# Attention and a gelu layer in one kernel: batch 1's first chunk asked for ahead, W_in in quarters, and another order of the first batch's steps

## The chip, the cores and the metric

The kernel runs on one core of one Trainium2 chip. Its time is the device time of one launch in microseconds. Before the change three runs took 426.42, 427.21 and 431.62 us; the median is 427.21. The core has a tensor engine (PE), a vector engine (DVE), a scalar engine (ACT), GpSimd (POOL) and a sync engine (SP). Each works through its own queue of instructions in order, and semaphores tie the queues together. Sixteen DMA engines carry the data.

## The reference

```python
q_n, k_n = (rmsnorm(q, g_q), rmsnorm(k, g_k))        # q, k, v: 8 batches x 12 heads x 448 tokens x 64
scores = scale * np.matmul(q_n, k_n.transpose(0, 1, 3, 2))
attn = np.exp(scores - np.max(scores, axis=-1, keepdims=True))
attn = attn / (np.sum(attn, axis=-1, keepdims=True) + 1e-09)
x = np.matmul(attn, v).transpose(0, 2, 1, 3).reshape(3584, 768)
h = x @ w_in                                          # 768 x 2048
g = 0.5 * h * (1.0 + np.tanh(c * (h + 0.044715 * h * h * h)))
out = g @ w_out                                       # 2048 x 768
```

All inputs and the output are float32. The kernel casts v and the weights to bfloat16 while they are loaded.

## The kernel before

Each batch goes through the same stages: q and k are squared, summed and normed (`square`, `total`, `rsqrt`, `normed`), transposed, multiplied to scores, and passed through an exponential; the exponentials are multiplied with v; the result x goes through the first matrix product and gelu; and the second matrix product of batch b runs inside the attention of batch b + 1, in whose queue its matmuls fill the gaps. A batch's twelve heads are cut into three chunks (`NCH`) of four heads, and a chunk into two pairs j = 0 and 1.

From batch 2 on these stages follow a regular plan. Batch 0 has nothing before it that could hide its loads and its norms, so its steps, and those that prepare batch 1, stand in a list written out by hand, `FRONT`. The function `front` carries out one step after the other, and each engine gets its instructions in the order of that list. A step is named by what it does and by a number; a letter behind a colon names the engine (A for ACT, D for DVE, P for POOL):

- `sq`, `sk` square a pair of q or of k of batch 0 (i = 2 x chunk + pair); `tq`, `tk` sum the squares on DVE; `rs` makes the reciprocal roots of both on ACT (a logarithm and an exponential); `nq`, `nk` multiply by them; `tpq`, `tpk` transpose on PE; `cq`, `ck` copy the transposed pair from PSUM to SBUF.
- `s0` to `s20` are the scores of batch 0, seven tiles for each chunk; `e0` to `e20` are their exponentials on ACT.
- For each of the six pairs of heads, `su` sums the exponentials on PE (by a product with ones), `st`, `rc`, `rb` transpose the sum, take its reciprocal and transpose it back on DVE, `xp` multiplies with v on PE, and `xt` scales the result on DVE. `su` writes the one bank of PSUM called o, which `st` frees.
- `z` puts idle products with zeros into PE's queue (z403: three of them, in the bank of pair 4).
- `ma`, `mc`, `md` are parts of the first matrix product, which reads `win` (W_in) two blocks of 128 columns at a time; `g0` to `g8` are the gelus.
- `v0`, `v1`, `v2` load batch 0's v: v0 its main part, v1 and v2 the last 64 tokens; `V0` to `V2` the same for batch 1. `w` loads a part of W_in's columns, `o0` to `o3` quarters of W_out. POOL issues all of these, among its own arithmetic.
- `L10`, `L11`, `L12` load chunks 0, 1, 2 of q and k of batch 1; SP issues them, six DMAs for a chunk.
- `Sq`, `Sk`, `Tq`, `Tk`, `Rs`, `Nq`, `Nk`, `Tp`/`TP`, `Cq`, `Ck` prepare batch 1 as the small letters do batch 0. `GELU` and `EXP` load ACT's tables, and `U` adds a third place in PSUM for scores.

The scores and the first product take turns in two, after `U` three, places in PSUM. Raw q and k have four buffers each (`rawqk`); before the list starts, batch 0's three chunks are loaded, and two pairs of tiles are allocated that nothing uses. The parts of W_in are loaded by `w_in_part(i, n)`, the i-th of n equal ranges of columns.

Of the kernel before, what the change touches and what calls it, by code (L numbers as in the profile page):

```python
# [8 lines left out]
F32 = mybir.dt.float32  # L9
# [7 lines left out]
def kernel(  # L17
# [12 lines left out]
    B, H, S, D = q.shape  # L30
# [21 lines left out]
    rawqk = ctx.enter_context(tc.tile_pool(name="rawqk", bufs=4))  # L52
# [29 lines left out]
    gcol = consts.tile([128, 1], F32)  # L82
# [3 lines left out]
    shift = consts.tile([128, 1], F32)  # L86
# [22 lines left out]
    def load_q(b, c):  # L109
        t = rawqk.tile([P, CH, NQ, D], F32, tag="rawq", name="rawq")  # L110
        raws["q", b, c] = t
        return [
            lambda j=j: nc.sync.dma_start(
                t[:, 2 * j:2 * j + 2],
                q[b, head(c, j):head(c, j) + 2].rearrange("h (p t) d -> p h t d", t=NQ),
            )
            for j in range(2)
        ]
# [6 lines left out]
    def load_k(b, c):  # L125
        t = rawqk.tile([128, 2, NS, D], F32, tag="rawk", name="rawk")
        raws["k", b, c] = t

        def main(j):
            h = head(c, j)  # L130
            nc.sync.dma_start(
                t[:, :, 4 * j:4 * j + NK],
                k[b, h:h + 2, :SM].rearrange("a (p t) d -> p a t d", t=NK),
            )

        def last(j):
            h = head(c, j)
            nc.sync.dma_start(t[own(j), :, NK], k[b, h:h + 2, SM:].rearrange("a p d -> p a d"))
# [25 lines left out]
    def sq_tile(n, flat):  # L164
        if n == "q":
            return flat[:P].rearrange("p (h t d) -> p h t d", h=CH, t=NQ)
        return flat[:, :2 * NS * D].rearrange("p (a s d) -> p a s d", a=2, s=NS)
# [29 lines left out]
    def total(b, c, n, j=None):  # L197
        nc.vector.reduce_sum(stat(ssq[b % 3], b, c, n, j), view(n, sqs[n, b, c], j), axis=AX.X)  # L198

    def rsqrt(b, c=slice(0, NCH), at=slice(0, NU)):  # L200
        if b not in rinvs:
            rinvs[b] = smp.tile([128, NCH, NU], F32, tag="rinv", name="rinv")
        lg = smp.tile([128, NCH, NU], F32, tag="lg", name="lg")
        nc.scalar.activation(
            lg[:, c, at], ssq[b % 3][:, c, at], AF.Ln, scale=1.0 / D, bias=eps
        )
        nc.scalar.activation(rinvs[b][:, c, at], lg[:, c, at], AF.Exp, scale=-0.5)  # L207
# [124 lines left out]
    def bank():  # L332
        return ps_o.tile([128, 512], F32, tag="o", name="o")
# [223 lines left out]
    nc.scalar.preload_act_table_set(EXP_SET)  # L557
    loads(0, 1)
    loads(0, 2)

    for _ in range(2):
        rawqk.tile([P, CH, NQ, D], F32, tag="rawq", name="rawq")
        rawqk.tile([128, 2, NS, D], F32, tag="rawk", name="rawk")
    nc.vector.memset(eps, 1e-6)
    nc.vector.memset(ones, 1.0)
    nc.vector.memset(rows, 1.0)
# [10 lines left out]
    free = g.rearrange("p f s -> p (f s)")  # L577
    for i, (n, c) in enumerate((n, c) for c in range(NCH) for n in "qk"):
        sqs[n, 0, c] = sq_tile(n, free[:, i * 2048:(i + 1) * 2048].bitcast(F32))

    def w_in_part(i, n):
        m = d_ff // n
        nc.gpsimd.dma_start(
            win[:, :, i * m:(i + 1) * m],
            moe_w_in[:, i * m:(i + 1) * m].rearrange("(c p) f -> p c f", p=128),
        )
# [34 lines left out]
    def front(step):  # L621
        what, _, eng = step.partition(":")
        name, i = what.rstrip("0123456789"), what[len(what.rstrip("0123456789")):]
        i, eng = int(i or 0), ENG.get(eng)
        c, j = i // 2, i % 2
        n = name[-1]
        if name in ("sq", "sk"):
            square(0, c, n, eng, ("pair", j))
        elif name in ("tq", "tk"):
            total(0, c, n, j)  # L630
        elif name == "rs":
            rsqrt(0, c, slice(14 * j, 14 + 16 * j))
        elif name in ("nq", "nk"):
            normed(0, c, n, j, eng)
        elif name in ("tpq", "tpk"):
            tps[n, i] = trans(0, i, n, turn[0], name)
        elif name == "cq":
            place_q(0, i, tps["q", i], eng)
        elif name == "ck":
            place_k(0, i, tps["k", i], eng)  # L640
        elif name == "U":
            third()
        elif name == "gcol":
            gains()
        elif name == "shift":
            shifts()
        elif name == "s":
            exps[i] = scores(0, *TILES[i])
        elif name == "e":
            exps[i]()  # L650
        elif name == "z":
            hp, m = divmod(i, 100)
            if hp not in sums_at:
                sums_at[hp] = bank()
            idle(m, sums_at[hp][:, :S])
        elif name == "su":
            pair_products(0, i, 0, sums_at.get(i))
        elif name == "st":
            recip_in()
        elif name == "rc":  # L660
            recip()
        elif name == "rb":
            recip_out(i)
        elif name == "xp":
            pair_products(0, i, 1, ps_m.tile([128, 512], F32, tag="mm", name="ox"))
        elif name == "xt":
            pair_x(0, i)
        elif name == "v":
            load_v(0, i)
        elif name == "w":  # L670
            w_in_part(i, 2)
        elif name == "V":
            load_v(1, i)
        elif name == "o":
            w_out_part(i // 2, slice(i % 2 * nf // 2, (i % 2 + 1) * nf // 2))
        elif name == "L":
            loads(*divmod(i, 10))
        elif name in ("Sq", "Sk"):
            square(1, i, n, eng)
        elif name in ("Tq", "Tk"):  # L680
            total(1, i, n)
        elif name == "Rs":
            rsqrt(1, slice(0, 2))
        elif name in ("Nq", "Nk"):
            normed(1, i // 10, n, i % 10, eng)
        elif name == "Tp":
            tps["Q", i] = trans(1, i, "q", ps_o, "o")
            tps["K", i] = trans(1, i, "k", ps_m, "mm")
        elif name == "TP":
            tp = place("tp").rearrange("p a s -> p (a s)").bitcast(BF16)  # L690
            tps["Q", i], tps["K", i] = (
                trans(1, i, n, tp[:, 1024 * a:1024 * (a + 1)]) for a, n in enumerate("qk"))
        elif name == "Cq":
            place_q(1, i, tps["Q", i], eng)
        elif name == "Ck":
            place_k(1, i, tps["K", i], eng)
        elif name in ("GELU", "EXP"):
            nc.scalar.preload_act_table_set(EXP_SET if name == "EXP" else GELU_SET)
        elif name in ("ma", "mc", "md"):
            fs = [2 * i, 2 * i + 1] if i < 7 else [i + 7]  # L700
            cs = {"ma": range(4), "mc": [4], "md": [5] if i < 3 else range(HP)}[name]
            mm1(0, fs, cs, act=False)
        elif name == "g":
            gelu(0, [2 * i, 2 * i + 1] if i < 7 else [i + 7])
        else:
            raise ValueError(step)

    FRONT = """
        sq0:A tq0 sk0:A tk0 sq1:P gcol rs0 shift nq0:P tq1 sk1:A tk1 tpq0 sq2:A v0 nk0:D rs1 cq0:D
        tpk0 tq2 sk2:A z3 v1 ck0:A tk2 v2 s0 nk1:D rs2 s1 w0 nq1:D e0 tpk1 sk3:D w1 tpq1 e1 s2 tk3  # L710
        z5 sq3:P ck1:D e2 cq1:D nk2:P tq3 s3 sq4:A s4 nq2:D rs3 tpk2 e3 tq4 nq3:P tpq2 z1 ck2:D e4
        cq2:D s5 nk3:D su0 e5 sk4:D L10 s6 tk4 sq5:P tpq3 e6 st0 tpk3 s7 sk5:P tq5 rs4 su1 rc0 e7
        rb0 nk4:P s8 ck3:D nq4:P s9 e8 st1 tpk4 cq3:D xp0 e9 ck4:D tk5 tpq4 xt0 s10 rs5 s11 cq4:D
        e10 xp1 nq5:P rc1 rb1 e11 s12 nk5:P xt1 su2 e12 L11 L12 s13 st2 tpq5 e13 tpk5 s14 rc2
        Sk0:P xp2 ck5:D e14 rb2 s15 xt2 su3 cq5:A Sq0:P e15 U Tk0 s16 xp3 e16 st3 s17 rc3 Tq0 s18
        e17 z403 rb3 e18 s19 su4 xt3 e19 s20 st4 xp4 e20 o0 rc4 rb4 ma0 GELU o1 xt4 Sq1:P su5 xp5
        V0 V1 st5 V2 Sk1:P rc5 mc0 rb5 ma1 xt5 Tq1 o2 o3 md0 mc1 Tk1 g0 md1 ma2 g1 EXP mc2 md2 md3
        Rs0 GELU Nq00:D Nk00:D Sk2:D g2 Tp0 md4 g3 Nk01:D Sq2:D Ck0:A Cq0:A Nk11:D md5 g4 Nq01:D
        Tq2 Nk10:P Nq10:P Tk2 Tp1 g5 Nq11:P md6 Ck1:D Cq1:A md7 g6 TP2 Ck2:D Cq2:D md8 TP3 Ck3:D
        Cq3:D g7 g8  # L720
"""
    for step in FRONT.split():
        front(step)
# [146 lines left out]
```

## Time and profile before

| | |
|---|---|
| median of three runs | 427.21 us (426.42 to 431.62) |
| the profiled execution | 429.53 us |
| its span, first to last instruction | 427.8 us |
| mean granted clock of PE | 0.992 |
| PE busy | 410.6 us, 96% of the span |
| ACT, DVE, POOL busy | 296.8, 279.0, 133.7 us |
| read from HBM, written to it | 45.61 MB, 11.01 MB |

The span and what lies around it (1.7 us) make the profiled execution's time. A busy share is an average over the whole span. The list `FRONT` covers the first 64 us of it, so the first 64 us are to be read on their own: which engine waits there, for whom, and what the DMA engines carry meanwhile.

### The profile page before, as it was taken

What the parts mean: (1) busy time and instruction counts of PE and PEld (TensorE: products, weight loads), DVE (VectorE), ACT (ScalarE), POOL (GpSimd) and SP (SyncE); (2) the same over time, 40 slices, a digit from 0 to 9 for tenths busy, and PEclk for the clock granted to TensorE, in tenths of its full rate; (3) what the DMA queues carried; (4) which work ended last, traced back from release to release, by engine and by line L of the source; (5) the groups of instructions that cost most, each with busy time, mean ns of one, the idle gap of its engine ahead of it and who ended that gap; (6) DMA issues with size and microseconds to landing.
All of it is one profiled execution on the core that took longest, in us unless ns stands there. A gap on an engine that the chain in (4) does not pass through costs nothing.

```text
span 427.8 us, 9133 instructions
## 1 busy us (share of the span) xinstructions
PE 410.6 (96%) x3733; PEld 232.7 (54%) x3733; DVE 279.0 (65%) x452; ACT 296.8 (69%) x400; POOL 133.7 (31%) x139
## 2 busy tenths in 40 slices
PE   7697999999999999999999999999999999999996
PEld 2232555565555655556555655556555655556563
DVE  5985676798769856787468836787387742683010
ACT  5786659678898678776877668776777558774300
POOL 6737660016000375009520375008430370000000
PEclk9988999999999999999999999999999999999999
DMA  8999998954991098915992097925972061120022
GB/s 194 222 225 231 203 199 158 220 152 100 174 251 41 2 181 202 167 53 116 196 181 73 14 201 142 188 61 104 199 103 71 10 124 38 43 72 2 0 76 74
DMA packets 96298, 54.15 MB, mean 127 GB/s; under 512 B 63744, under 2 KB 91264, under 8 KB 96256
## 3 DMA queue, kind: packets, MB, share of 16 engines
q1 hardware_dynamic: 71392, 41.67, 42.9%
q0 software_dynamic: 24544, 11.80, 21.1%
q8 instruction: 29, 0.48, 0.5%
q10 hardware_dynamic: 320, 0.10, 0.1%
q14 instruction: 13, 0.11, 0.1%
HBM read 45.61 MB, written 11.01 MB: 132 GB/s over the span
## 4 chain that ended last, share of the span: by engine, by line
PE 81%; DMA 7%; ACT 5%; DVE 5%; issue 1%; SPq 1%; POOL 0%; DVEq 0%; ACTq 0%; POOLq 0%
PE o L418 33%; PE hh L391 25%; PE o L349 10%; DMA rawk<-in_k_dram 7%; PE sc L312 6%; PE h L391 4%; PE sc L302 1%; ACT g L400 1%; ACT ex L316 1%; DVE ss L198 1%; DVE sq L183 1%; ACT exr L316 1%; DVE es L328 1%; ACT sq L181 1%; DVE st L356 1%
## 5 line engine op out<-in xcount | busy, mean ns | idle before, releaser
L418 PE MATMUL o<-wout,g 128*64 128x384 bf16 (+1 forms) x1664 | 157.8, 326 | 0.0
L316 ACT ACTIVATE ex<-sc,shift 128x896 bf16<-128x896 f32 x144 | 136.2, 1013 | 6.4 <-PE sc L312 6.4
L391 PE MATMUL hh<-xT,win 128*64 128x448 bf16 (+1 forms) x924 | 133.2, 353 | 0.1
L418 PEld LDWEIGHTS <-g 128*64 128x64 bf16 (+1 forms) x1664 | 98.7, 109 | 49.1 <-issue 3.8
L391 PEld LDWEIGHTS <-win 128*64 128x64 bf16 (+1 forms) x1062 | 86.2, 105 | 59.1 <-issue 3.6
L400 ACT ACTIVATE g<-hh 128x896 bf16<-128x896 f32 x56 | 49.4, 916 | 48.7 <-PE hh L391 48.7
L198 DVE TENSOR_REDUCE ss<-sq 128x14 f32<-128x896 f32 (+2 forms) x43 | 47.4, 1124 | 30.4 <-ACT sq L181 18.5
L440 ACT COPY osb<-o 128x384 f32<-128x384 f32 x51 | 24.7, 484 | 49.2 <-PE o L418 49.1
L727 POOL COPY mark<-es 1x1 bf16<-1x1 bf16 x6 | 1.1, 178 | 170.2 <-DVE es L330 170.2
L356 DVE STREAM_TRANSPOSE st<-o 128x448 f32<-128x448 f32 x48 | 31.1, 648 | 28.2 <-PE o L349 28.1
L221 POOL TENSOR_TENSOR nrmq<-rawq,rinv 112x512 bf16<-112x512 f32 x36 | 38.8, 1093 | 6.0 <-ACT rinv L207 6.0
L312 PE MATMUL sc<-qT,kT 64*128 64x448 bf16 x288 | 39.4, 358 | 1.3 <-ACT exr L316 0.8
L330 DVE TENSOR_TENSOR es<-ex 128x896 bf16<-128x896 bf16 x42 | 26.3, 627 | 17.6 <-ACT ex L316 17.6
L221 POOL TENSOR_TENSOR nrmk<-rawk,rinv 128x384 bf16<-128x384 f32 (+1 forms) x34 | 35.4, 1055 | 5.0 <-issue 3.4
L349 PE MATMUL o<-ex,vb 128*64 128x448 bf16 x252 | 31.2, 353 | 1.2 <-DVE st L356 1.2
L364 DVE STREAM_TRANSPOSE rb<-rc 128x448 f32<-128x448 f32 x48 | 30.9, 645 | 1.6
L274 DVE TENSOR_SCALAR kT<-kT,gcol 128x896 bf16<-128x896 bf16 x19 | 21.8, 1146 | 13.4 <-DMA kT<-nrmk 13.4
L328 DVE TENSOR_TENSOR es<-es,exr 64x896 bf16<-64x896 bf16 x42 | 26.0, 618 | 3.0 <-ACT exr L316 1.6
L330 DVE TENSOR_TENSOR es<-es,ex 128x896 bf16<-128x896 bf16 x42 | 25.6, 609 | 2.6 <-ACT ex L316 0.7
L374 DVE TENSOR_TENSOR xT<-o,rb 128x448 bf16<-128x448 f32 x42 | 25.9, 616 | 0.7
L316 ACT ACTIVATE exr<-sc,shift 128x896 bf16<-128x896 f32 x24 | 24.5, 1019 | 0.6 <-PE sc L302 0.5
L312 PEld LDWEIGHTS <-kT 64*128 64x128 bf16 x288 | 10.1, 94 | 25.1 <-issue 19.3
(79 smaller groups left out, 333.3 us busy)
## 6 DMA issues: line engine op xcount, KB each, us to landing
rawq<-in_q_dram SPq DMA_DIRECT2D x48, 224.0 KB, 4.3
rawk<-in_k_dram SPq DMA_DIRECT2D x48, 192.0 KB, 4.6
vb<-in_v_dram POOLq DMA_DIRECT2D x8, 576.0 KB, 9.3
win<-in_moe_w_in_dram POOLq DMA_DIRECT2D x2, 1536.0 KB, 24.8
wout<-in_moe_w_out_dram POOLq DMA_DIRECT2D x4, 768.0 KB, 15.0
out_dram<-osb SPq DMA_DIRECT2D x7, 336.0 KB, 3.5
out_dram<-osb SPq DMA_DIRECT2D x8, 288.0 KB, 2.7
out_dram<-osb SPq DMA_DIRECT2D x8, 240.0 KB, 2.7
```

The source lines that it names most:

```text
L198: nc.vector.reduce_sum(stat(ssq[b % 3], b, c, n, j), view(n, sqs[n, b, c], j), axis=AX.X)
L221: eng.tensor_mul(dst.rearrange("p t a d -> p a t d"), view(n, raws[n, b, c], j), r.to_broadcast(list(r.shape) + [D]),)
L312: nc.tensor.matmul(sc[:, a, :S], kT[r, c, 4 * j + t], qT[b][r, hp], start=True, stop=True,)
L316: return lambda: nc.scalar.activation(dst, sc[:, :, :S], AF.Exp, scale=scale, bias=shift)
L328: nc.vector.tensor_add(es[p], es[p], exrs[b, hp // 2][p])
L330: nc.vector.tensor_add(es, ex[:, 0] if t == 1 else es, ex[:, t])
L349: nc.tensor.matmul(o[a * D:(a + 1) * D], w(a), e[:, a], start=(i == 0), stop=(i + 1 == len(steps)),)
L356: nc.vector.transpose(oas["st"].rearrange("p a b -> p (a b)"), oas[0])
L364: nc.vector.transpose(oas["rb", hp], oas["rc"].to_broadcast([128, S // 32, 32]))
L391: nc.tensor.matmul(h[i * m:(i + 1) * m, j, :S], win[:, c // 2 + NCH * (c % 2), f * 128 + i * m:f * 128 + (i + 1) * m], xT[b][:, c], start= ...
L400: nc.scalar.activation(g[:, fs[0]:fs[0] + len(fs), (b % 2) * S:(b % 2 + 1) * S], hs1[fs[0]][:, :, :S], AF.Gelu_apprx_tanh)
L418: nc.tensor.matmul(o[j * m:(j + 1) * m, :HD], g[:, f, i * 128 + j * m:i * 128 + (j + 1) * m], wout[:, f, half * HD:(half + 1) * HD], start ...
```

## The change

Batch 1's first chunk, `loads(1, 0)`, is asked for right behind batch 0's three chunks instead of by the step `L10` in the list; the two pairs of unused tiles go. W_in is loaded in four parts of 512 columns instead of two of 1024. v1 and v2 stand ahead of v0. The list is another one: the same kinds of steps, with other engines for some and in another order.

```diff
     loads(0, 1)
     loads(0, 2)
-
-    for _ in range(2):
-        rawqk.tile([P, CH, NQ, D], F32, tag="rawq", name="rawq")
-        rawqk.tile([128, 2, NS, D], F32, tag="rawk", name="rawk")
+    loads(1, 0)
...
+    NW = 4
...
         elif name == "w":
-            w_in_part(i, 2)
+            w_in_part(i, NW)
...
     FRONT = """
-        sq0:A tq0 sk0:A tk0 sq1:P gcol rs0 shift nq0:P tq1 sk1:A tk1 tpq0 sq2:A v0 nk0:D rs1 cq0:D
-        tpk0 tq2 sk2:A z3 v1 ck0:A tk2 v2 s0 nk1:D rs2 s1 w0 nq1:D e0 tpk1 sk3:D w1 tpq1 e1 s2 tk3
-        z5 sq3:P ck1:D e2 cq1:D nk2:P tq3 s3 sq4:A s4 nq2:D rs3 tpk2 e3 tq4 nq3:P tpq2 z1 ck2:D e4
-        cq2:D s5 nk3:D su0 e5 sk4:D L10 s6 tk4 sq5:P tpq3 e6 st0 tpk3 s7 sk5:P tq5 rs4 su1 rc0 e7
-        rb0 nk4:P s8 ck3:D nq4:P s9 e8 st1 tpk4 cq3:D xp0 e9 ck4:D tk5 tpq4 xt0 s10 rs5 s11 cq4:D
-        e10 xp1 nq5:P rc1 rb1 e11 s12 nk5:P xt1 su2 e12 L11 L12 s13 st2 tpq5 e13 tpk5 s14 rc2
-        Sk0:P xp2 ck5:D e14 rb2 s15 xt2 su3 cq5:A Sq0:P e15 U Tk0 s16 xp3 e16 st3 s17 rc3 Tq0 s18
-        e17 z403 rb3 e18 s19 su4 xt3 e19 s20 st4 xp4 e20 o0 rc4 rb4 ma0 GELU o1 xt4 Sq1:P su5 xp5
-        V0 V1 st5 V2 Sk1:P rc5 mc0 rb5 ma1 xt5 Tq1 o2 o3 md0 mc1 Tk1 g0 md1 ma2 g1 EXP mc2 md2 md3
-        Rs0 GELU Nq00:D Nk00:D Sk2:D g2 Tp0 md4 g3 Nk01:D Sq2:D Ck0:A Cq0:A Nk11:D md5 g4 Nq01:D
-        Tq2 Nk10:P Nq10:P Tk2 Tp1 g5 Nq11:P md6 Ck1:D Cq1:A md7 g6 TP2 Ck2:D Cq2:D md8 TP3 Ck3:D
-        Cq3:D g7 g8
+        sq0:P sk0:A tq0 tk0 sq1:P gcol rs0 shift nq0:P tq1 sk1:A nk0:D v1 tpq0 sq2:A tk1 tpk0 v2
+        cq0:D rs1 v0 ck0:D sk2:A tq2 s0 s1 sq3:A nk1:D z1 e0 nq1:D tpk1 tk2 w0 L11 tpq1 e1 s2
+        ck1:D z1 sk3:P cq1:D rs2 tq3 s3 e2 z3 nq2:D e3 tk3 nk2:P s4 tpq2 sk4:P tpk2 rs3 cq2:D s5
+        ck2:D e4 su0 nk3:P tk4 e5 s6 nq3:D tpk3 st0 sk5:P L12 e6 tpq3 s7 ck3:D e7 sq4:P cq3:D s8
+        rc0 su1 rb0 e8 sq5:P tq4 s9 xp0 st1 e9 w1 tq5 s10 rs4 w2 s11 xt0 e10 rc1 w3 xp1 tk5 e11
+        rb1 nq4:P su2 xt1 rs5 s12 nk4:P st2 s13 e12 tpq4 nq5:P tpk4 rc2 xp2 cq4:D e13 ck4:D nk5:P
+        rb2 s14 tpq5 xt2 e14 s15 Sq0:P tpk5 cq5:D su3 ck5:D e15 U s16 st3 xp3 Sk0:P e16 rc3 rb3
+        s17 s18 e17 xt3 z403 Tk0 e18 su4 Tq0 s19 s20 e19 ma0 st4 o0 rc4 e20 rb4 xp4 o1 Sq1:P GELU
+        su5 xt4 Sk1:A xp5 st5 V0 V1 V2 rc5 mc0 rb5 ma1 xt5 Tk1 o2 o3 md0 mc1 Tq1 g0 md1 ma2 g1 EXP
+        mc2 md2 md3 Rs0 GELU Nk10:D Nq01:D Nk11:D g2 md4 Nk00:D g3 Nq00:D Nk01:D Nq11:D Tp0 g4
+        Nq10:P md5 Ck0:D Cq0:D Sq2:P Tp1 g5 Sk2:P md6 Tq2 Ck1:A Cq1:A Tk2 md7 g6 TP2 Ck2:D Cq2:D
+        md8 TP3 Ck3:D Cq3:D g7 g8
 """
```

## The prediction

> **What bounds the kernel now.** I read the page first, then the chain of waits, then the timeline of the first 65 us, the busy time by stage, and the DMA queues.
>
> ```profile
> span 427.8 us, 9133 instructions
> ```
>
> The change touches only the first 64 us: batch 0's attention, its first matrix product, batch 1's preparation. From the chain of waits, and from the timeline, the rows around 36 us and at the stage's end:
>
> ```profile
> 16.21 16.88 DMA rawk<-in_k_dram
> ```
> ```profile
> 33.21 1.68 POOL L183 TENSOR_TENSOR sq<-rawk 128x896 f32<-128x896 f32 x1 [4.46 <-DMA rawk<-in_k_dram]
> ...
> 34.92 1.09 DVE L198 TENSOR_REDUCE ss<-sq 128x14 f32<-128x896 f32 x1 [2.84 <-POOL sq L183]
> ...
> 36.62 1.28 PE L212 MATMUL o<-zeros 128*128 128x448 bf16 x3 [2.25 <-DVE st L356]
> ...
> 39.91 0.36 PE L312 MATMUL sc<-qT,kT 64*128 64x448 bf16 x2
> ```
> ```profile
> 64.32 4.09 PE L418 MATMUL o<-wout,g 128*64 128x384 bf16 x48
> ```
>
> A column is start, duration, engine, line, tiles; the bracket is idle time before it and who ended it. Read it as one stall. Batch 1's first k chunk lands at 33.1 after 16.9 us; POOL squares it (step Sk0); DVE waits 2.84 us for the square, because its row sum Tk0 stands in DVE's queue ahead of st3; PE waits 2.25 us for st3, which frees the bank for z403 and su4; behind those stand s19 and s20, the last scores of batch 0 (39.91). From s20 to the first product with W_out (64.32), which opens batch 1's attention, there are 24.4 us, in which PE hardly rests:
>
> ```profile
> 0.00:10.00 10.00, 7.11 (x29) 3.01 (x30) 5.01 (x18) 5.08 (x11) 6.56 (x17) 1.00 0.79 193
> 10.00:20.00 10.00, 6.75 (x54) 2.78 (x52) 9.96 (x15) 7.64 (x13) 8.02 (x9) 1.00 1.33 220
> ...
> 40.00:50.00 10.00, 10.00 (x64) 4.84 (x64) 6.44 (x10) 5.38 (x6) 7.32 (x7) 1.00 1.27 209
> 50.00:64.00 14.00, 13.39 (x93) 7.27 (x91) 10.60 (x14) 9.35 (x14) 9.75 (x6) 1.00 1.46 197
> ```
>
> (Columns: stretch, length, then busy time of PE, weight loads, DVE, ACT, POOL, the granted clock, the DMA share, GB/s.) PE is busy 10.00 of 10 us and 13.39 of 14, the DMA engines throughout. So what s20 gains is carried to the end nearly whole, and before s20 ACT's exponentials e0 to e20 set the pace. Its rows there:
>
> ```profile
> 11.26 1.89 ACT L316 ACTIVATE ex<-sc,shift 128x896 bf16<-128x896 f32 x2
> 14.73 1.01 ACT L316 ACTIVATE ex<-sc,shift 128x896 bf16<-128x896 f32 x1 [1.58 <-PE sc L312]
> 15.64 0.62 ACT L181 ACTIVATE g<-rawq 112x512 f32<-112x512 f32 x1
> 16.60 0.31 ACT L204 ACTIVATE lg<-ss,eps 128x16 f32<-128x16 f32 x1 [0.34 <-DVE ss L198]
> 16.94 0.22 ACT L207 ACTIVATE rinv<-lg 128x16 f32<-128x16 f32 x1
> ...
> 21.76 0.31 ACT L204 ACTIVATE lg<-ss,eps 128x14 f32<-128x14 f32 x1 [1.01 <-DVE ss L198]
> ...
> 24.21 1.91 ACT L316 ACTIVATE ex<-sc,shift 128x896 bf16<-128x896 f32 x2 [1.01 <-PE sc L312]
> ...
> 27.11 1.01 ACT L316 ACTIVATE exr<-sc,shift 128x896 bf16<-128x896 f32 x1 [0.50 <-PE sc L302]
> 28.02 3.69 ACT L316 ACTIVATE ex<-sc,shift 128x896 bf16<-128x896 f32 x4
> 31.58 0.56 ACT L248 COPY qT<-tp 128x448 bf16<-128x448 bf16 x1
> ...
> 38.42 1.01 ACT L316 ACTIVATE ex<-sc,shift 128x896 bf16<-128x896 f32 x1 [2.40 <-PE sc L312]
> 40.31 1.01 ACT L316 ACTIVATE ex<-sc,shift 128x896 bf16<-128x896 f32 x1 [0.88 <-PE sc L312]
> ```
>
> From e0 (11.26) to e20's start (40.31) are 29.05 us: 20 exponentials at 0.92 (3.69 for four) are 18.4; three reciprocal roots (rs3 to rs5) at 0.31 + 0.22 and a gap, 0.57 each, are 1.7; a square and a copy 0.62 + 0.56 = 1.2; the brackets sum to 7.7. That is 29.0, so the ledger closes.
>
> **Part 1: the early request for batch 1's first chunk (L10).** It should do nothing by itself. SP issues nothing but loads here, in the same order before and after, each behind the landing of the eighth before it. The two placeholder tiles taken out held no one up:
>
> ```profile
> 14.66 2.15 SPq L138 DMA_DIRECT2D rawk<-in_k_dram  x2
> ```
>
> This already issues L10's last pieces, so its place in the list cost nothing. L11 now reuses chunk 0's buffers and L12 chunk 1's, as before. Cost 0.
>
> **Part 2: W_in in quarters, v's last tokens first.** The rows of the queues, of issues and of sizes:
>
> ```profile
> 10.66 1.68 POOL L583 DMA_DIRECT2D win<-in_moe_w_in_dram  x2
> ```
> ```profile
> q0 software_dynamic: 992, 2.00, 87.6%
> q1 hardware_dynamic: 993, 0.69, 24.2%
> ```
> ```profile
> rawq<-in_q_dram SPq DMA_DIRECT2D x48, 224.0 KB, 4.3
> rawk<-in_k_dram SPq DMA_DIRECT2D x48, 192.0 KB, 4.6
> vb<-in_v_dram POOLq DMA_DIRECT2D x8, 576.0 KB, 9.3
> win<-in_moe_w_in_dram POOLq DMA_DIRECT2D x2, 1536.0 KB, 24.8
> ...
> rawk<-in_k_dram SPq DMA_DIRECT2D x48, 32.0 KB, 4.6
> ...
> vr<-in_v_dram POOLq DMA_DIRECT2D x16, 48.0 KB, 10.1
> ```
>
> The queue rows are of 22 to 34 us: W_in (q0) moves 2.00 MB while q and k (q1) get 0.69, a quarter. Now one quarter (768 KB) goes out at about 10.7 and the other three only after sq5 on POOL, about 22 in the walk below. Ahead of L10's end then stand four chunks of 2 x (224 + 192 + 32) = 896 KB, v's 576 + 2 x 48, and 768: 5024 KB or 5.14 MB. The first 10 us move 1.93 (193 GB/s), the rest at 220 takes 14.6: L10 lands near 24.6, with some of the second quarter beside it near 25.5, against 33.1.
>
> The Trainium skill (DMA: Bandwidth & Descriptors, section Queues, rings and completion order) has each DMA engine take its queues in turn, a packet of up to 64 descriptors at a time. By that rule W_in's share depends on packets and not on row length, and after 22 us L11 and L12 crawl at a quarter as before. That costs at most part 4's small slack; the sum doesn't rest on it.
>
> W_in's need: in the walk its second quarter is first read at about 42 (ma2), the last at about 52 (md6). At 2.00 MB per 12 us a quarter takes 4.7, at half that rate 9.4: from 22 the second lands between 27 and 31, the last between 36 and 50. No wait is expected; the cover is 2 us at worst, and gone it costs PE what is missing. Shorter rows may also move more slowly: 197 GB/s (50 to 64 us, W_out's rows of half the length) against 220 for 3.1 MB is 1.7 us of DMA time. It falls on W_out:
>
> ```profile
> 36.68 1.82 POOL L589 DMA_DIRECT2D wout<-in_moe_w_out_dram  x2
> ```
> ```profile
> DMA to landing us min/median/max: 12.2/15.0/17.8
> ```
>
> Its first half lands by 55.4 even at the longest, used at 64.32, or 59 now: 1.9 left after the 1.7. POOL pays two more issues (2 x 0.84). Only eight of POOL's DMAs may be in flight too: o2 now waits for the second quarter and o3 for the third. Behind o3 stand Nq10, Sq2 and Sk2 on POOL, which batch 1's last transposes need at about 55. The third lands by 41 at the slow rate: cost 0, up to the slack of some 10 us.
>
> **Part 3: the order on the engines up to s20.** These rows show what the move of squares from ACT and DVE to POOL may cost:
>
> ```profile
> 11.72 2.24 DVE L221 TENSOR_TENSOR nrmq<-rawq,rinv 112x512 bf16<-112x512 f32 x1
> ...
> 13.32 1.93 POOL L221 TENSOR_TENSOR nrmk<-rawk,rinv 128x384 bf16<-128x384 f32 x1
> ...
> 16.48 0.68 DVE L221 TENSOR_TENSOR nrmq<-rawq,rinv 112x512 bf16<-112x512 f32 x1
> ...
> 22.39 0.83 POOL L221 TENSOR_TENSOR nrmk<-rawk,rinv 128x384 bf16<-128x384 f32 x1 [1.67 <-ACT rinv L207]
> 23.18 1.04 POOL L221 TENSOR_TENSOR nrmq<-rawq,rinv 112x512 bf16<-112x512 f32 x1
> ```
>
> Alone such a product takes 0.68 on DVE and 0.83 to 1.04 on POOL; side by side 2.24 and 1.93. The Trainium skill (SBUF — State Buffer, section Who interferes with whom) lets a DVE instruction with two SBUF inputs and a GpSimd instruction that reads SBUF block each other, the later one until the first has ended. The rows agree; the lower bound below is what full blocking would give.
>
> ACT loses from this stretch sq4 (0.62) and the copy cq5 (0.56) and takes in rs2 (0.57, now behind e1): 18.4 + 4 x 0.57 = 20.7 us of work, from an e0 that stays at 11.3 (sq0 on POOL is hidden: nq0 stands behind sq1 there in both lists, and sq1 waits for its data). I walked the list, engine by engine, with the durations of these rows. The first two waits as an example: ck0 ends at 10.4, then DVE makes tq2 (to 11.1), nk1 and nq1, both stretched (12.1, 13.3), and tk2 (13.9), while e1 ends at 13.2, so rs2 waits 0.7; tq3 ends at 15.4, nq2, stretched, at 16.4, tk3 at 17.1, while e3 ends at 16.4, so rs3 waits 0.7. The others: e12 for s12, behind xp1 and su2 on PE, 0.6; e14 for ck4, whose product nk4 POOL makes after the three W_in issues, 0.3; e16 and e17 behind su3 and xp3, 0.5; e19 behind su4, 0.4. Together 3.2, an estimate, against 7.7. The stall's brackets (2.40 and 0.88) are all but gone by order alone: Tk0 and Tq0 now stand behind st3, rc3, rb3 and xt3, so they hold back st4 at most. In the walk Sk0 ends at 32.3 and DVE comes to Tk0 at 33.1. If L10 still landed at 33.1, Sk0 would end at 34.9, and st4 and su5 would lose about 0.8.
>
> e20 then starts at 11.3 + 20.7 + 3.2 = 35.2, against 40.31: **5.1 us**; s20, one place of PSUM ahead of e20, goes at about 34.6, 5.3 earlier. Bounds: the waits on PE (1.1) are queued work and stay, so at most 5.1 + 2.1 = 7.2; if each of DVE's four products on POOL's path waits for a whole 1.04 us instruction, where the walk has 1.65 in all, 4.2 - 1.65 = 2.5 is lost, leaving 2.6. I take the middle, since only one of the pairs quoted overlapped fully.
>
> Four of twelve idle products (z) go. The row at 36.62 shows the price of an idle PE: 1.28 / 3 = 0.43 each after a rest of 2.25, where s20's two take 0.36. The walk has no rest so long. Cost 0; bounds: 4 x 0.43 = 1.7 gained, which ACT hides, or one more such slow stretch, in which su and xp cost about 1 more.
>
> **Part 4: from s20 to batch 1's attention.** PE's 24.4 us are the same instructions. DVE now makes seven of batch 1's eight early products (0.68 or less) and no squares; Sq2 and Sk2 go to POOL, Sk1 to ACT, which waits for PE there. Tp0 needs the fifth product, 0.68 x 5 = 3.4 us after the roots, and PE has md2 to md4 in front of it. Cost 0, bound 1.3 (a late L11 under Sk1).
>
> **The sum.** 429.53 in the profiled execution (span 427.8 and 1.7 around it) becomes 424.4. That run lies 2.3 above the median of 427.21; from the median, **422.1**.
>
> **The rivals.** *DVE becomes the bound* (0.20): it is busy 9.96 of 10 us already from 10 to 20, and anything late there is passed to ACT. If the new list waits as long as the old, 7.7 for 3.2, the gain is 0.6: 426.6. For it: 9.96; against: the squares sk3 and sk4 leave DVE, and the largest brackets were the stall's. *POOL becomes the bound, slower* (0.10): sk3 to nq4 are eight products in POOL's queue. If each is stretched as the row of 1.93 was, by 1.1, nq4 ends some 7.1 later than walked, net of what is charged, and e14 and all behind it too: 5.1 - 7.1 = -2.0, or 429.2. It ends on the slower side once the stretch exceeds 5.1. For it: 1.93; against: DVE has four such products there, not eight. *The request changes nothing and L10 stays late* (within the forecast, see parts 1 and 3): 0.8 less, 422.9. *More than the bound* (0.08), if ACT runs nearly without waits: 5.1 + 3.2 = 8.3, or 418.9.
>
> **Numbers.** Forecast 0.62, its own range 420.0 (7.2 gained) to 424.6 (2.6). Eight in ten needs the first rival too and leaves the slower one out: 419 to 427.5. Two per cent, about what a measurement of this kernel can tell from no change, is 8.5 us: faster than 418.7 takes more than half of the last case, 0.05; over 435.8 the slower rival at more than four times its price, 0.03; the rest 0.92.
>
> **What would show it.** Right: rawk of L10 lands before 28; no bracket over 1 us before e19 and e20; s20 near 34.6 and the first product with W_out near 59; everything after shifted alike. Wrong: POOL's nq4 after 30, DVE without a gap and xt3 after 37, PE waiting at ma2 to md7 for W_in, POOL stuck before o3, or the granted clock at half in stretches where it was full.

## The result, and the profile after

| | before | after |
|---|---|---|
| median (lowest to highest) | 427.95 us (425.10 to 431.95, 20 runs) | 424.67 us (423.67 to 427.88, 20 runs) |
| ratio, 95% interval | | 0.9926 (0.9900 to 0.9952) |
| profiled execution, its span | 429.53, 427.8 us | 423.7, 421.9 us |
| mean granted clock of PE in it | 0.992 | 0.996 |
| start of the first product with W_out (L418) | 64.32 us | 58.04 us |
| from there to the end of the span | 363.5 us | 363.9 us |

The kernel became faster by 3.3 us, or 0.74%. The last two rows say where: all of the gain is made ahead of the first product with W_out, and what follows takes as long as before. This holds in every profile of this study. In the fourteen of them the stretch from that product to the end takes 363.4 to 364.1 us, while its start moves between 56.1 and 67.1 us. The start of the first L418 is therefore the number to compare between profiles. Runs over 1.5% above the fastest of the same kernel (six of the 75 of before that were timed beside the experiments, two of e1_request) count as slow and are left out of the ratios.

The timeline of the kernel after, around the places that the prediction quoted of before (start, duration, engine, line, tiles; the bracket is the idle time before and who ended it; here and in the fences below, rows in between are left out):

```profile
28.45 1.67 POOL L183 TENSOR_TENSOR sq<-rawk 128x896 f32<-128x896 f32 x1
30.33 2.20 DVE L198 TENSOR_REDUCE ss<-sq 128x14 f32<-128x896 f32 x2
31.30 0.55 PE L312 MATMUL sc<-qT,kT 64*128 64x448 bf16 x4
31.71 1.91 ACT L316 ACTIVATE ex<-sc,shift 128x896 bf16<-128x896 f32 x2 [0.23 <-PE sc L312]
...
42.67 1.53 DVE L221 TENSOR_TENSOR nrmq<-rawq,rinv 112x512 bf16<-112x512 f32 x1
43.62 3.40 POOL L183 TENSOR_TENSOR sq<-rawq 112x1024 f32<-112x1024 f32 x1
45.19 2.38 DVE L221 TENSOR_TENSOR nrmq<-rawq,rinv 112x512 bf16<-112x512 f32 x1
46.98 2.73 POOL L183 TENSOR_TENSOR sq<-rawk 128x896 f32<-128x896 f32 x1
47.63 0.37 PE L233 MATMUL tp<-ident,nrmq 112*128 112x112 bf16 x4 [1.67 <-DVE nrmq L221]
48.10 2.16 DVE L221 TENSOR_TENSOR nrmq<-rawq,rinv 112x512 bf16<-112x512 f32 x1
50.94 0.37 PE L233 MATMUL tp<-ident,nrmq 112*128 112x112 bf16 x4 [0.50 <-DVE qT L250]
...
58.04 4.09 PE L418 MATMUL o<-wout,g 128*64 128x384 bf16 x48
```

The stall is gone. POOL squares batch 1's first k (28.45) without a wait, since it had landed at 25.8; the row sums (30.33) wait for nothing; s19 and s20 run together at 31.30, and e20, the second of the two exponentials from 31.71, starts at 32.6, where before it was 40.31. A new loss stands in the lower part. Three of DVE's products for batch 1 are stretched: one takes 1.53 us beside POOL's product Nq10, two take 2.38 and 2.16 us beside POOL's two squares of chunk 2 (Sq2, Sk2). PE waits 1.67 us and 0.50 us at batch 1's transposes.

The busy time by stage shows the same. Columns: stretch, length, busy time of PE, weight loads, DVE, ACT, POOL, granted clock, DMA share, GB/s:

```profile
10.00:20.00 10.00, 9.17 (x66) 3.60 (x64) 9.32 (x20) 9.63 (x15) 8.49 (x9) 0.83 1.32 224
...
40.00:50.00 10.00, 8.33 (x50) 4.33 (x49) 7.81 (x7) 6.02 (x8) 7.71 (x4) 1.00 1.29 206
50.00:64.00 14.00, 13.10 (x126) 7.45 (x125) 8.02 (x15) 10.46 (x15) 2.05 (x3) 1.00 1.47 197
```

From 10 to 20 us PE is busy for 9.17 of 10 us where it was 6.75, and ACT for 9.63 where it was 7.64. From 40 to 50 PE is busy for only 8.33 where it was 10.00: that is the new loss. The DMA queues from 22 to 34 us (packets, MB, share of 16 engines) show batch 1's chunks coming faster, 1.13 MB where it was 0.69:

```profile
q0 software_dynamic: 1600, 1.61, 78.7%
q1 hardware_dynamic: 1763, 1.13, 40.3%
```

### The profile page after: what moved, and what is told of

It is laid out like the page before. It is cut to its first block, busy times and chain, and to the rows that moved or that the text cites. A ratio compares the mean times of both kernels' runs of the same rounds, so it can differ in the third digit from the quotient of the medians.

```text
span 421.9 us, 9128 instructions
## 1 busy us (share of the span) xinstructions
PE 408.2 (97%) x3729; PEld 232.5 (55%) x3729; DVE 277.1 (66%) x453; ACT 295.6 (70%) x397; POOL 135.4 (32%) x143
## 4 chain that ended last, share of the span: by engine, by line
PE 71%; issue 12%; DMA 5%; ACT 4%; DVE 4%; POOL 3%; SPq 1%; POOLq 0%; ACTq 0%; DVEq 0%
PE o L418 29%; PE hh L391 20%; PE o L349 9%; PE sc L312 6%; PE h L391 3%; DMA vb<-in_v_dram 3%; ACT ex L316 2%; DVE nrmq L221 1%; PE ox L349 1%; PE sc L302 1%; DMA rawk<-in_k_dram 1%; DMA rawq<-in_q_dram 1%; POOL nrmq L221 1%; ACT g L400 1%; POOL vr L154 1%
## 5 line engine op out<-in xcount | busy, mean ns | idle before, releaser
L418 PE MATMUL o<-wout,g 128*64 128x384 bf16 (+1 forms) x1664 | 157.8, 326 | 0.0
L418 PEld LDWEIGHTS <-g 128*64 128x64 bf16 (+1 forms) x1664 | 98.9, 109 | 48.7 <-issue 3.7
L356 DVE STREAM_TRANSPOSE st<-o 128x448 f32<-128x448 f32 x48 | 31.1, 647 | 25.8 <-PE o L349 25.6
L330 DVE TENSOR_TENSOR es<-ex 128x896 bf16<-128x896 bf16 x42 | 26.5, 632 | 17.2 <-ACT ex L316 17.1
L221 POOL TENSOR_TENSOR nrmq<-rawq,rinv 112x512 bf16<-112x512 f32 x34 | 35.1, 1045 | 4.1 <-issue 2.5
L221 POOL TENSOR_TENSOR nrmk<-rawk,rinv 128x384 bf16<-128x384 f32 (+1 forms) x34 | 31.9, 954 | 1.1 <-ACT rinv L207 1.1
L183 POOL TENSOR_TENSOR sq<-rawq 112x1024 f32<-112x1024 f32 x9 | 18.6, 2061 | 27.5 <-DMA rawq<-in_q_dram 23.9
```

Source lines behind the costliest of these rows:

```text
L221: eng.tensor_mul(dst.rearrange("p t a d -> p a t d"), view(n, raws[n, b, c], j), r.to_broadcast(list(r.shape) + [D]),)
L330: nc.vector.tensor_add(es, ex[:, 0] if t == 1 else es, ex[:, t])
L356: nc.vector.transpose(oas["st"].rearrange("p a b -> p (a b)"), oas[0])
L418: nc.tensor.matmul(o[j * m:(j + 1) * m, :HD], g[:, f, i * 128 + j * m:i * 128 + (j + 1) * m], wout[:, f, half * HD:(half + 1) * HD], start ...
```

## The experiments

Every kernel was timed in rounds with the kernel before, four kernels to a group on one chip, three groups. The kernel before had medians of 430.49, 430.21 and 430.37 us in them, above the 427.95 of the first measurement. "L418" is the start of the first product with W_out in the profile, "L10" and "L11" the landing of the last k piece of batch 1's first two chunks, all in us.

| run | median (lowest to highest, runs) | ratio, 95% interval | L10 | L11 | L418 |
|---|---|---|---|---|---|
| e1_request | 429.58 (426.24 to 433.08, 12) | 0.9992 (0.9948 to 1.0035) | 33.6 | 41.7 | 65.84 |
| e2_dma | 425.12 (424.60 to 425.84, 6) | 0.9889 (0.9835 to 0.9943) | 26.4 | 35.2 | 60.37 |
| e3_list | 432.17 (431.08 to 433.90, 12) | 1.0058 (1.0022 to 1.0094) | 31.0 | 43.5 | 67.14 |
| e4_act | 421.64 (421.31 to 422.63, 6) | 0.9814 (0.9765 to 0.9863) | 26.9 | 35.3 | 56.77 |
| after_again | 424.73 (424.07 to 427.63, 6) | 0.9895 (0.9840 to 0.9950) | 26.8 | 34.8 | 62.31 |
| e5_idle | 421.85 (421.29 to 423.56, 6) | 0.9822 (0.9766 to 0.9879) | 26.6 | 35.2 | 56.13 |
| e6_list_sk1 | 432.71 (431.28 to 433.99, 12) | 1.0060 (1.0029 to 1.0092) | 30.4 | 42.6 | 66.71 |
| e7_quarters_early | 426.37 (424.39 to 429.24, 12) | 0.9944 (0.9903 to 0.9984) | 28.2 | 37.9 | 61.67 |
| e8_list_act | 426.24 (425.76 to 426.94, 12) | 0.9925 (0.9892 to 0.9958) | 30.7 | 42.6 | 60.75 |
| e9_v_first | 426.72 (424.26 to 428.42, 12) | 0.9931 (0.9888 to 0.9973) | 25.4 | 34.8 | 59.17 |
| e10_act_v_first | 422.37 (421.27 to 422.64, 6) | 0.9822 (0.9766 to 0.9877) | 26.8 | 33.8 | 56.59 |
| e11_half_late | 431.88 (429.97 to 432.69, 12) | 1.0052 (1.0015 to 1.0090) | 32.5 | 42.2 | 64.72 |

### The parts alone: the request, the transfers, the list

**e1_request**: the kernel before with the request for batch 1's first chunk in its new place, and nothing else.

```diff
     loads(0, 2)
-    for _ in range(2):
-        rawqk.tile([P, CH, NQ, D], F32, tag="rawq", name="rawq")
...
+    loads(1, 0)
...
-        cq2:D s5 nk3:D su0 e5 sk4:D L10 s6 tk4
+        cq2:D s5 nk3:D su0 e5 sk4:D s6 tk4
```

> The kernel before with the early request alone: L10 taken out of the list and asked for behind batch 0's chunks, the unused tiles gone. Theory A (the request does nothing, the order of SP's queue is the same): ratio to before 1.000 within 0.003, batch 1's first k chunk lands near 33, s20 near 40. Theory B (the request is what moves the chunk ahead): it lands before 28 and the stall ahead of e19 goes, ratio 0.993 or lower.

No difference, and L10 lands at 33.6 as before. The request by itself does nothing.

**e2_dma**: the list of before with the changed transfers.

```diff
-            w_in_part(i, 2)
+            w_in_part(i, 4)
...
-        sq2:A v0 nk0:D
+        sq2:A v1 nk0:D
...
-        sk2:A z3 v1 ck0:A tk2 v2 s0
+        sk2:A z3 v2 ck0:A tk2 v0 s0
...
-        e0 tpk1 sk3:D w1 tpq1
+        e0 tpk1 sk3:D tpq1
...
-        s7 sk5:P tq5
+        s7 sk5:P w1 w2 w3 tq5
```

> The kernel before with the DMA part alone: W_in in quarters, the last three behind sk5 on POOL, v's last tokens first; the list's order of arithmetic stays. Theory A (the order of the list makes the gain, the transfers only part of it): the chunk lands near 26, POOL's Sk0 no longer waits, the 2.8 us of DVE and the 2.4 and 0.9 us of ACT go, s20 near 37, the early waits stay; some 2 to 3 us less than before in the profile. Theory B (the transfers make the gain): as much as the whole change, s20 near 32, 6 us less in the profile.

The transfers alone give 0.9889, which the whole change does not beat clearly (0.9895 in after_again). ACT has no bracket before e19 and e20, s20 starts at 35.96, and the first L418 at 60.37, 24.4 us later, as long as before:

```profile
35.96 0.36 PE L312 MATMUL sc<-qT,kT 64*128 64x448 bf16 x2
...
60.37 4.09 PE L418 MATMUL o<-wout,g 128*64 128x384 bf16 x48
```

**e3_list**: the changed list, with W_in in two halves asked for together as before.

```diff
-    NW = 4
+    NW = 2
...
-        tpk1 tk2 w0 L11
+        tpk1 tk2 w0 w1 L11
...
-        e9 w1 tq5 s10 rs4 w2 s11 xt0 e10 rc1 w3 xp1
+        e9 tq5 s10 rs4 s11 xt0 e10 rc1 xp1
```

> The changed kernel with W_in in two halves at its old place: the new list alone. Theory A (order): batch 1's first k chunk lands near 33 again and Tk0 waits for it, but behind st3, so s20 stays near 32 and st4 and su5 lose 1 to 3 us; ratio to before 0.993 to 0.998. Theory B (transfers): the gain goes, s20 back near 38 and ratio 1.00.

The new order, with the early request and the order of v that belong to it, is slower than before by 0.6%. Up to s20 it does what it does in the changed kernel: the pair s19 and s20 starts at 32.07, and the bracket before e19 is 0.23. Then everything is given back, as the timeline of this run shows:

```profile
43.57 0.95 ACT L181 ACTIVATE sq<-rawk 128x896 f32<-128x896 f32 x1 [7.89 <-DMA rawk<-in_k_dram]
49.54 3.40 POOL L183 TENSOR_TENSOR sq<-rawq 112x1024 f32<-112x1024 f32 x1
51.11 4.01 DVE L221 TENSOR_TENSOR nrmq<-rawq,rinv 112x512 bf16<-112x512 f32 x1
52.90 1.67 POOL L183 TENSOR_TENSOR sq<-rawk 128x896 f32<-128x896 f32 x1
55.18 0.56 PE L233 MATMUL tp<-ident,nrmq 112*128 112x112 bf16 x4 [5.10 <-DVE nrmq L221]
```

Two things are to be seen: ACT stands 7.89 us before Sk1, because L11's k lands only at 43.5, and one product of DVE takes 4.01 us while POOL makes two squares, with PE waiting 5.10 us behind it. Which of the two costs more is not to be read from this profile. The next runs part them.

### POOL's squares beside DVE's products

**e4_act**: the changed kernel with Sq2 and Sk2 on ACT.

```diff
-        Nk00:D g3 Nq00:D Nk01:D Nq11:D Tp0 g4 Nq10:P md5 Ck0:D Cq0:D Sq2:P Tp1 g5 Sk2:P md6
+        Nk00:D g3 Sq2:A Nq00:D Nk01:D Nq11:D Tp0 g4 Sk2:A Nq10:P md5 Ck0:D Cq0:D Tp1 g5 md6
```

> The changed kernel with batch 1's two last squares (Sq2, Sk2) on ACT, behind g3 and g4, instead of POOL. Theory C (the two squares on POOL stretch DVE's products and make PE wait for Tp0 and Tp1): DVE's products of 1.5 to 2.4 us fall to about 0.7, PE's 1.67 and 0.50 us of waiting go, the first product with W_out at about 56 in place of 58.0, some 2 us less than the changed kernel. Theory D (the late roots behind the table load set Tp0): PE still waits over 1 us before Tp0 and the time is that of the changed kernel.

The products that stood beside the squares fall back to 0.68 us (the one beside Nq10 still takes 1.53), and ACT makes the first square in 1.06 us, where POOL took 1.9 undisturbed:

```profile
46.18 1.06 ACT L181 ACTIVATE sq<-rawq 112x1024 f32<-112x1024 f32 x1
46.29 0.68 DVE L221 TENSOR_TENSOR nrmq<-rawq,rinv 112x512 bf16<-112x512 f32 x1
46.89 0.68 DVE L221 TENSOR_TENSOR nrmk<-rawk,rinv 128x512 bf16<-128x512 f32 x1
47.03 0.37 PE L233 MATMUL tp<-ident,nrmq 112*128 112x112 bf16 x4
47.49 0.68 DVE L221 TENSOR_TENSOR nrmq<-rawq,rinv 112x512 bf16<-112x512 f32 x1
```

PE waits for no product any more. From s20 (32.6, the second half of the pair at 32.40) to the first L418 (56.77) are 24.2 us, the length of before. The time falls to 421.64 us, about 3 us below the changed kernel, and its six runs scatter by 1.3 us. All six lie below the fastest of the changed kernel's 26 runs (423.67), so this version beats both kernels.

**after_again**: the changed kernel unaltered, beside the next three.

> The changed kernel unaltered, as the base for the three runs beside it. If the first measurement stands, about 424 to 425 us and a ratio of 0.985 to 0.995; if before's larger scatter on a chip decides the ratio, the time stays near 424.5 while the ratio moves with the median of before.

The time repeats to 0.06 us; the ratio moves with before. This profile, of a run of 427.63 us, shows where the same program can lose time:

```profile
32.92 0.55 PE L312 MATMUL sc<-qT,kT 64*128 64x448 bf16 x4
...
44.29 3.39 DVE L221 TENSOR_TENSOR nrmq<-rawq,rinv 112x512 bf16<-112x512 f32 x1
45.24 1.88 POOL L183 TENSOR_TENSOR sq<-rawq 112x1024 f32<-112x1024 f32 x1
47.09 3.19 POOL L183 TENSOR_TENSOR sq<-rawk 128x896 f32<-128x896 f32 x1
48.67 2.16 DVE L221 TENSOR_TENSOR nrmq<-rawq,rinv 112x512 bf16<-112x512 f32 x1
50.89 0.37 PE L233 MATMUL tp<-ident,nrmq 112*128 112x112 bf16 x4 [3.31 <-DVE nrmq L221]
```

Here DVE's first product lost against POOL (3.39 us) and POOL's first square did not (1.88); in the first profile it was 1.53 and 3.40. Of the 4.3 us by which the first L418 comes later than in the first profile, 1.6 lie ahead of the pair s19 and s20 (32.92 instead of 31.30) and 2.7 behind it. PE's wait is 3.31 us instead of 1.67 and 0.50, and a stretch of half clock follows it: the granted clock from 50 to 58 us is 0.79 in the busy time by stage.

```profile
50.00:58.00 8.00, 7.11 (x40) 3.68 (x41) 4.78 (x7) 1.92 (x3) 2.62 (x4) 0.79 1.51 194
```

**e6_list_sk1**: e3_list with Sk1 on POOL.

```diff
-        su5 xt4 Sk1:A xp5
+        su5 xt4 Sk1:P xp5
```

> The changed list with W_in in two halves at its old place (as in the run e3_list), but step Sk1 on POOL and not on ACT. Leaves nothing out. Theory A, e3_list lost its 7 to 8 us because ACT stood 7.9 us before g0 for L11's k, with PE's products on W_out's input behind it: now g0 runs on time, PE's wait of 1.6 us for g and part of the later waits go, but Rs0 still waits for the square of a chunk that lands at 43.5, so the scores start late: 427 to 430 us. Theory B, the landing at 43.5 alone sets the time whatever engine squares it: no change, 431 to 433 us. Theory C, the order is the whole gain and Sk1 the whole loss: 424 to 425 us.

The time does not move, as the second theory had it, though the next run shows that its reason, the landing alone, was wrong. ACT's first gelu now runs at 40.14, ahead of L11's landing, but the late roots bring a product into the middle of POOL's work:

```profile
47.89 5.79 DVE L221 TENSOR_TENSOR nrmq<-rawq,rinv 112x512 bf16<-112x512 f32 x1
48.56 1.09 POOL L221 TENSOR_TENSOR nrmq<-rawq,rinv 112x512 bf16<-112x512 f32 x1
49.56 1.93 POOL L183 TENSOR_TENSOR sq<-rawq 112x1024 f32<-112x1024 f32 x1
51.41 1.71 POOL L183 TENSOR_TENSOR sq<-rawk 128x896 f32<-128x896 f32 x1
55.41 0.55 PE L233 MATMUL tp<-ident,nrmq 112*128 112x112 bf16 x4 [7.80 <-DVE nrmq L221]
```

POOL's three instructions follow each other and take their usual times; DVE's one product lasts until all three are through. PE waits 7.80 us.

**e8_list_act**: e3_list with Sq2 and Sk2 on ACT, the edit of e4_act.

> The changed list with W_in in two halves at its old place (as in the run e3_list, 432.2 us), with Sq2 and Sk2 on ACT behind g3 and g4 in place of POOL. Leaves nothing out. In e3_list one product of DVE took 4.01 us beside POOL's two squares and PE waited 5.10 us for it. Theory A, that stretch is a cost of its own on top of the late landing of L11: the products go back to 0.68 us, Tp0 and Tp1 come 3.3 us earlier, 428 to 429.5 us. Theory B, the landing of L11 at 43.5 us sets the time and the stretch hides behind it: 431 to 433 us.

It gains 5.9 us over e3_list, more than either theory had it, though L11 lands as late (42.6) and ACT still stands 7.38 us before Sk1. The products behind Nq10 take 0.68 us, PE waits 1.77 us for one of them where it was 5.10, and the granted clock is 1.00 from 40 to 58 us, where e3_list had half clock from 52.9 to 59.8.

```profile
51.01 0.37 PE L233 MATMUL tp<-ident,nrmq 112*128 112x112 bf16 x4 [1.77 <-DVE nrmq L221]
```

So the two squares on POOL, with the wait and the half clock behind them, cost 5.9 us when the chunks land late, and 3.1 us when they land early (e4_act). The late chunks cost 4.6 us with the squares on ACT (426.24 against 421.64) and 7.5 with them on POOL (432.17 against 424.67): the two losses make each other larger.

### W_in: quarters or lateness

**e7_quarters_early**: the changed kernel with all four quarters asked for together, where the two halves were.

```diff
-        tpk1 tk2 w0 L11
+        tpk1 tk2 w0 w1 w2 w3 L11
...
-        e9 w1 tq5 s10 rs4 w2 s11 xt0 e10 rc1 w3 xp1
+        e9 tq5 s10 rs4 s11 xt0 e10 rc1 xp1
```

> The changed kernel with all four quarters of W_in asked for together at about 10.7 us, where its two halves were asked for before. Theory A, the share of W_in in the queues depends on the number of its packets and not on the length of its rows, so only the later request of three quarters helped: L10's last k lands at 31 to 33 us and L11's at 42 to 44, ACT stands before Sk1, 430 to 432 us. Theory B, rows of half the length halve W_in's share as long as other queues have work, so quarters help wherever they are asked for: L10's last k lands at 27 to 30, L11's at 35 to 38, 424 to 426 us. Between the two, a time of 426 to 430 with both at work.

**e11_half_late**: the changed kernel with two halves, the second asked for at the place of the second quarter.

```diff
-    NW = 4
+    NW = 2
...
-        e9 w1 tq5 s10 rs4 w2 s11 xt0 e10 rc1 w3 xp1
+        e9 w1 tq5 s10 rs4 s11 xt0 e10 rc1 xp1
```

> The changed kernel with W_in in two halves, the second asked for where the second quarter is now (about 20 us): late, but with rows of 2 KB. The fourth corner beside e3_list (halves, early, 432.2 us), e7_quarters_early (426.4 us) and the changed kernel (quarters, late, 424.7 us). Theory A, the row length sets the shares while W_in's queue holds anything, and from 10.7 us on it always does: L10's last k lands near 30 and L11's at 41 to 43, 430 to 432 us. Theory B, asking late is worth as much by itself: L10's last k before 27, L11's at 37 to 39, 425 to 427 us.

The four corners, with the same list in all (median time; landing of L10 and L11):

| | asked for together | last part or parts late |
|---|---|---|
| halves (rows of 2 KB) | 432.17 us; 31.0, 43.5 | 431.88 us; 32.5, 42.2 |
| quarters (rows of 1 KB) | 426.37 us; 28.2, 37.9 | 424.67 us; 25.8, 35.0 |

Cutting the rows gives 5.8 or 7.2 us, the late request 0.3 or 1.7, which the intervals of the ratios, overlapping in both rows, do not tell from nothing. The queues of 22 to 34 us show what the rows do. First e11_half_late, then e7_quarters_early:

```profile
q0 software_dynamic: 996, 2.01, 88.0%
q1 hardware_dynamic: 995, 0.65, 23.6%
```
```profile
q0 software_dynamic: 1623, 1.63, 79.9%
q1 hardware_dynamic: 1625, 1.08, 38.9%
```

The two queues move the same number of packets, 996 to 995 and 1623 to 1625, as they did before (992 to 993). A packet of W_in is one row: 2.01 MB / 996 is 2.0 KB, 1.63 MB / 1623 is 1.0 KB. With rows half as long, W_in gives way to q and k in bytes, whenever it is asked for. The changed kernel's 1600 to 1763 are not equal: from 26 to 34 us they are (1083 to 1084), but from 22 to 26 W_in's queue moves only 517 to 679. Why it moves fewer there stays open.

### Idle products and the order of v

**e5_idle**: e4_act with seven more idle products.

```diff
-        sk2:A tq2 s0 s1 sq3:A nk1:D z1 e0
+        sk2:A tq2 z4 s0 s1 sq3:A nk1:D z4 e0
```

> The changed kernel with Sq2 and Sk2 on ACT (as in the run e4_act) and seven more idle products on PE: four ahead of s0 and four instead of one behind s1. Theory A, the half-clock stretch from about 12 to 16 us starts because PE idles in the first 11 us, and ACT waits for nothing there, so more idle products take it away: granted clock full from 10 to 20 us, e20 starts up to 1 us earlier, 420.6 to 421.3 us. Theory B, the idle products are queued work on PE and push s2 and the transposes back without changing the clock: the half stretch stays, e1 and e2 wait for their scores, 421.6 to 423 us. Theory C, the stretch is hidden behind the exponentials anyway: clock full and no change, 421.6 us.

The clock is full from 10 to 20 us (1.00 where the changed kernel had 0.83 and e4_act, too, had a half-clock stretch), and the median is that of e4_act within 0.2 us. This fits the third theory, that the early half-clock stretch is hidden behind the exponentials, but a few tenths are not excluded: in the two profiles with the new list and no such stretch (e5_idle, e8_list_act) s19 and s20 start at 31.76 and 31.74, in the nine with one between 31.30 and 32.92.

**e9_v_first** is the changed kernel, **e10_act_v_first** e4_act, with v's main part ahead of its last tokens again.

```diff
-        nk0:D v1 tpq0 sq2:A tk1 tpk0 v2
+        nk0:D v0 tpq0 sq2:A tk1 tpk0 v1
...
-        cq0:D rs1 v0 ck0:D
+        cq0:D rs1 v2 ck0:D
```

> The changed kernel with v's main part asked for ahead of its last tokens, as before the change. Theory A, the order of v matters only through xp0's wait of 0.5 us for v: v's main part lands about 1 us earlier, the wait goes, 424.2 to 424.7 us. Theory B, the last tokens asked for later make s2's neighbours or L10 late: over 425.5 us. Theory C, no effect: 424.7 us.

> As e9_v_first, and with Sq2 and Sk2 on ACT as in the run e4_act (421.6 us). The candidate for the fastest version. If the two edits add, 421.1 to 421.6 us; if the order of v does nothing, 421.6 us; if v's last tokens become late, over 422.5 us.

In e9_v_first v's main part lands at 18.2 instead of 20.5, and L10 at 25.4. Both runs are slower than their counterparts, by 2.0 and 0.7 us, but they were timed in another group, and the intervals of the ratios overlap with those of after_again and e4_act. What the order of v is worth is not settled by this; to undo it brought no gain, and e4_act stays the fastest.

## Why the prediction was right, and where it was not

**What bounds the kernel.** Right. The stage up to the first L418 sets the time, and what follows moves as a block.

**Part 1, the request.** Right: cost 0 by e1_request. L10's delay did not come from when it was asked for.

**Part 2, the transfers.** The landing of L10 was forecast for 25.5 and came at 25.8 (26.8 in after_again). No wait for W_in by PE is in the profile after; o3 waits 1.85 us for a part of it, at no cost, as said. The step that failed is the one on L11 and L12, that they "crawl at a quarter as before" and that this "costs at most part 4's small slack". The shorter rows end the crawl (L11 at 35.0, where the halves have 42.2 to 43.5), and where it stays, in e3_list and e11_half_late, the kernel is 7 us slower than the changed one, not 1.3. The Trainium skill (DMA: Bandwidth & Descriptors, section Queues, rings and completion order) has an engine go from queue to queue at the bounds of packets. The counts above agree with turns of equal numbers of rows. From that the prediction drew that the share does not depend on row length, which is the wrong way round: with equal numbers of rows the bytes follow their length. e8_list_act shows what late chunks cost by themselves: 426.24 us against e4_act's 421.64, 4.6 us between kernels that differ in W_in's parts alone.

**Part 3, up to s20.** The mechanism was right and its size too small. s20 came at 31.5 instead of 34.6, 8.4 us earlier than before and not 5.3. The term that was mis-sized is the sum of waits: 3.2 us were walked from the rows of before, and the brackets after sum to 1.2 us (0.29, 0.26, 0.20, 0.19 and the 0.23 quoted above). Of these 0.9 are waits for PE, for which the forecast had 1.1; the others, forecast at 2.1, came to 0.3. Work of 20.7 us plus 1.2 from an e0 at 10.65 gives 32.55 for e20, and 32.6 was measured. e0 itself came 0.6 us earlier, which the forecast kept at 11.3, so e20 came 7.7 us earlier and passed the bound of 7.2. Of the eleven profiles with this list this one has the earliest s20: in after_again s20 came at 33.1, 1.5 us ahead of the forecast and not 3.1. That the stall goes "by order alone" is shown by e3_list, and that it also goes by transfers alone, by e2_dma. But the 0.8 us put on a late L10 was low. In e11_half_late, with L10 at 32.5, DVE waits 3.10 us for the square again and PE 1.99 us for st4, and a half-clock stretch follows.

**Part 4, from s20 on.** This step failed: "Cost 0, bound 1.3". From s20 to the first L418 the changed kernel takes 26.5 us, 2.1 more than the 24.4 kept for it, and PE's two waits (1.67 + 0.50) are these 2.1; in after_again 3.31 us are waited. DVE's products were charged at "0.68 or less", though Sq2 and Sk2 had just been moved to POOL beside them, and part 3 had quoted the rows of 2.24 and 1.93 for a product of DVE beside one of POOL. e4_act, which takes the squares off POOL, brings it back to 24.2 and gains 3 us. The Trainium skill (SBUF — State Buffer, section Who interferes with whom) says that of two such instructions the later is blocked for the whole of the first; the row of 5.79 us shows more than this, since one DVE product was kept back through three POOL instructions in a row, though its record begins 0.7 us ahead of the first of them.

**The sum.** Part 3 brought 3.1 us more and part 4 took 2.1 of it, so the forecast of 424.4 us for the profiled execution met 423.7 by two errors of opposite sign. That is luck: the execution profiled in after_again, of the same program, needed 29.2 us from s20 to the first L418 and took 427.63. The median was forecast from 427.21, the middle of three runs, as 422.1, and is 424.67: 0.1 us above the forecast's own range and inside the whole range. Of the 2.6 us between them 0.7 lie in the basis (20 runs of before have a median of 427.95) and 1.8 in the gain, which is 3.3 us and not 5.1; in after_again's group it is 5.5. The gain differs so much because the runs of before scatter. They can be sorted by their granted clock: of the 69 runs of before beside the experiments that the ratios count, 30 had a mean clock of 0.99 or more, with a median of 426.9 us, and 39 a lower one, with 431.2. Of 26 runs of the changed kernel 21 had 0.99 or more (median 424.3) and 5 less (427.6). At like clocks the change is worth 2.6 and 3.6 us; the rest, up to the 5.5, fits the changed kernel's fewer runs at a lower clock. That the lower clock alone makes those runs long is not shown. The 18 runs of e4_act, e5_idle and e10_act_v_first, in whose profiles PE's long waits are gone, all had 0.99 or more.

**The rivals.** "DVE becomes the bound" did not come true where it was put: ahead of e20 the waits fell to 1.2 us instead of staying at 7.7. DVE held PE up in another place, beside Sq2 and Sk2. "POOL becomes the bound" did not come true either; nq4, for which the limit of 30 was named, starts at 22.80, and POOL's last product of batch 0 at 25.60. One of the signs of being wrong did show, a lower clock in a stretch where it was full: 0.83 from 10 to 20 us, where before had 1.00 (and 0.83 from 20 to 30). e5_idle took it away from e4_act, whose median did not move.

## What to carry to other kernels

When a step moves to GpSimd, price VectorE's two-input products that will run beside it at the stretched durations of the trace, not at those they have alone, and look behind them for who waits. When two queues share the DMA engines, compare packet counts and bytes: with equal counts, the queue with the longer rows takes the bytes, and cutting its rows hands them to the other. And three runs do not place the median of a kernel whose runs scatter by their clock.

## What the runs showed of the hardware

- A VectorE product of 0.68 us took up to 5.79 us beside GpSimd's products and squares; the longest began 0.7 us ahead of three GpSimd instructions and ended 0.6 us, about its own length, after the last of them (53.7 and 53.1 us in e6_list_sk1). Which engine lost differed between executions of the same program (after and after_again).
- Between 35 and 400 us a half-clock stretch of PE stood in each profile in which PE had waited 1.99 us or more there (e11_half_late; 2.25 in before, 3.54 in e1_request, 3.30 to 7.80 in e7_quarters_early, after_again, e3_list and e6_list_sk1), and in none in which its longest wait was 1.77 us or less. Ahead of 35 us the longest wait does not sort them so: in before a stretch stands between 20 and 30 us (clock 0.83), where PE's longest wait was 1.76 us. The length of the stretch did not follow the wait: it was 3.4 us after the 2.25 of before and the 3.31 of after_again, and 6.8 us after the 3.54 of e1_request and the 1.99 of e11_half_late (clock 0.80 and 0.52 from 35 to 40 and from 40 to 45 us). The busy time by stage of before, then of e1_request:

```profile
36.00:40.00 4.00, 3.38 (x15) 0.57 1.12 245
```
```profile
30.00:40.00 10.00, 6.46 (x47) 2.25 (x42) 5.36 (x8) 6.10 (x8) 5.30 (x4) 0.79 1.13 234
40.00:50.00 10.00, 10.00 (x60) 4.36 (x57) 6.44 (x10) 3.89 (x4) 7.70 (x7) 0.87 1.26 210
```

  (The first row has PE's busy time alone ahead of the clock.) A clock of 0.57 over 4 us is 0.43 x 4 x 2 = 3.4 us at half, and after_again's 0.79 over 8 us is 0.21 x 8 x 2 = 3.4; 0.21 and 0.13 short over 10 us each are 0.34 x 10 x 2 = 6.8 us.
